# A residual block on one core: nesting the columns of the last chunk's outer row positions, with merged nesting and output operations

## Chip, cores and metric

The kernel runs on one core of a Trainium2 chip. The metric is the device time of one execution in microseconds, as a median of several executions.

## The reference

The block is GroupNorm, SiLU and a 3x3 convolution, done twice, with a time embedding added in between and the input added at the end. x is 2 x 512 x 64 x 64, all data bf16.

```python
def reference(x, t_emb, g1, be1, w1, w_emb, g2, be2, w2):
    ...
    h = conv3(_silu(gn(x, g1, be1)), w1)         # 3x3, 512 -> 512 channels
    emb = _silu(t_emb) @ w_emb
    h = h + emb.reshape(B, C, 1, 1)
    h = conv3(_silu(gn(h, g2, be2)), w2)
    return x + h
```

## The kernel before

The work is cut into eight *chunks*, one for each layer (0 or 1), image and half image; chunks 0 to 3 are layer 0, chunks 4 to 7 layer 1. A chunk has four *units*, one for each block of 128 output channels, named here by chunk and block: unit 5,3 is the last of chunk 5. While TensorE works on the units of chunk c, VectorE and ScalarE produce the operands of chunk c+1 (`prod`: load, SiLU, transforms).

Rows are transformed so that four output rows come from six *row positions*: the inner ones 0 to 3 and the outer ones 4 and 5. For each position and each of the four input-channel blocks (`ct`) the column direction is done in one of two ways:

- plain: three matmuls of 512 columns, one for each column of the 3x3 filter;
- *nested*: the columns are transformed as well. Four matmuls of 256 columns are left, two of them (`B_mms`) on sums and two (`A_mms`) on differences. This asks VectorE for the differences and sums (the four nesting operations below) and for sums of the weights.

In chunks 4 to 7 the inner positions are nested and the outer ones plain, with weights that are streamed in for each unit.

```python
def plain_mms(bank, c, k, ct, s):                 # 3 matmuls x 512 columns
    ...
def B_mms(bank, c, k, ct, s):                     # 2 x 256, on the sums
    ...
def A_mms(bank, c, k, ct, s):                     # 2 x 256, on the differences
    ...
# rows_b: the nesting of one input-channel block (nf = 2 or 4 positions)
X = lambda i: A(xb + i, [[RW, 8 * nf], [1, 32]])
for kind, (i, j, op) in enumerate(((32, 33, SB_), (1, 0, SB_), (33, 0, SB_), (33, 0, AD))):
    s0 = vnest(c, ct, kind, 0)
    tt(A(s0, [[1, 256 * nf]]), X(i), X(j), op, nm)
```

A unit of chunks 4 to 7, and what every unit does after its matmuls:

```python
p1, p2, p3, p4 = next_pair(), next_pair(), next_pair(), next_pair()   # PSUM bank pairs, 3 in turn
run([(6, 4, plain_mms)]);  evac_o(4, 6)                   # outer: banks 6 and 7
run([(p1, 0, B_mms), (p1 + 1, 2, B_mms)]);  evac_b(0, p1)  # ScalarE empties PSUM
run([(7, 5, plain_mms)]);  evac_o(5, 7)
run([(p2, 1, B_mms), (p2 + 1, 3, B_mms)]);  evac_b(1, p2)
s_ops()                                                   # VectorE
run([(p3, 0, A_mms), (p3 + 1, 2, A_mms)]);  evac_pair(0, p3)
run([(p4, 1, A_mms), (p4 + 1, 3, A_mms)]);  evac_pair(1, p4)
... # sums into MB and SD
yr = lambda r0: A(ys + r0 * RW, [[RW, 16], [33, 2], [1, 32]])
tt(yr(0),  A(MB, [[0, 2], [1, 512]]), A(MB + 1024, [[512, 2], [1, 512]]), AD, nm + "y")     # reads MB
tt(yr(16), A(SD, [[0, 2], [1, 512]]), A(SD + 1024, [[-512, 2], [1, 512]]), AD, nm + "y")    # reads SD
```

Almost everything in on-chip memory lies in one tile, the *arena* `ar`; `A(offset, dims)` is a strided view of it (offsets in f16 elements of a partition).

```python
Z    = 60096   # scratch; SD0 = Z + 10016 (chunks 0-3), SD1 = Z + 12768 (chunks 4-7), O0 at Z + 11552
VB1  = 74944   # operands of the odd chunks
AB   = 91584   # the two row buffers: loads of x and h land here, SiLU works on them in place
YS   = 96004   # the two output buffers
MB   = 100164  # inner sums
```

The order on each engine is not written by hand. Each operation is registered with a `Plan`, which keeps the exact set of elements that it reads and writes, finds the dependencies from those sets, and makes a list schedule with a cost model of its own. The operations are then emitted in that order, and the framework below inserts the semaphore waits, by its own reading of the views:

```python
def op(self, eng, cost, fn, r=(), w=(), ...):
    for sp, idx in r: deps.update(np.unique(self.spaces[sp][0][idx]).tolist())   # exact elements
    ...
def emit(self):
    for o in sorted(self.ops, key=lambda o: (o.start, o.i)): o.fn()
```

## Time and profile before

| | before |
|---|---|
| time, median of 3 | 476.97 us (476.17 to 478.6) |
| span of the profiled execution | 474.9 us |
| TensorE busy, VectorE busy | 461.3, 428.2 us |
| TensorE's gaps after its opening 10 us | 4.2 us (1.26 + 1.72 + 0.86 + 0.32) |
| from TensorE's last matmul to the end of the span | 4.8 us |

The page of the profile: busy time of each engine (PE is TensorE, DVE VectorE, ACT ScalarE), the clock granted to TensorE in 40 slices, and the chain that ended last.

```profile
span 474.9 us, 8229 instructions
...
PE 461.3 (97%) x2936; PEld 283.4 (60%) x2936; DVE 428.2 (90%) x847; ACT 371.9 (78%) x580; POOL 38.8 (8%) x66
...
PEclk9998999999999999999999999999999999999999
...
PE 40%; DVE 24%; ACT 7%; issue 4%; POOL 0%; DVEq 0%; ACTq 0%; POOLq 0%
```

The timeline of TensorE, the stretches that begin after an idle time: start, length, operation, and in brackets the idle time before it and its releaser (the wait for the first load at the start is left out).

```profile
37.12 13.14 PE L379 MATMUL psum<-ar 128*128 128x512 f16 x51 [1.26 <-DVE ar L328]
91.86 12.15 PE L379 MATMUL psum<-ar 128*128 128x512 f16 x60 [1.72 <-ACT ar L351]
177.10 111.05 PE L379 MATMUL psum<-ar 128*128 128x512 f16 x642 [0.86 <-DVE fs L441]
289.49 180.64 PE L379 MATMUL psum<-ar 128*128 128x512 f16 x1292 [0.32 <-DVE fs L441]
```

TensorE is the limit: it runs without a gap from 289.5 to 470.1 us. It is also the largest part of the chain (40%, on the page); VectorE's 24% lie before 289.5 us and after 457.9 us, in the output work of the last unit. L328 is the helper for VectorE's two-operand operations, L351 the one for ScalarE, and L379 the one for matmuls.

Busy times in the first one and a half units of chunk 7 and in the rest of it: window, its length, busy us and count of PE, PEld, DVE, ACT and POOL, TensorE's clock, DMA share and GB/s.

```profile
420.00:439.00 19.00, 19.00 (x132) 12.65 (x130) 14.07 (x22) 12.21 (x16) 2.65 (x3) 1.00 0.53 116
439.00:475.00 36.00, 31.13 (x230) 22.26 (x228) 20.75 (x40) 14.58 (x17) 3.61 (x3) 1.00 0.42 82
```

VectorE is 74% busy in the first window (14.07 of 19 us) and 58% in the second (20.75 of 36): in chunk 7 there is room to give VectorE work that takes columns off TensorE. Two groups of VectorE operations by shape: count, busy us, mean ns, idle before them.

```profile
L328 DVE TENSOR_TENSOR ar<-ar 128x1024 f16<-128x1024 f16 x272 | 179.1, 692 | 11.4 <-ACT ar L351 10.7
...
L328 DVE TENSOR_TENSOR ar<-ar 128x2048 f16<-128x2048 f16 x15 | 18.3, 1219 | 7.0 <-ACT ar L351 7.0
```

The Trainium skill ("VectorE: DVE Perf Modes", the perf-mode tier table) has 1224 ns for a bf16 `tensor_tensor` of 2048 elements; these f16 ones take 1219, so the trace agrees. "Perfetto Trace Analysis" (Optimizing Scalar/DVE Operations) names an overhead of about 60 ns for each VectorE operation on on-chip memory and says that larger operations help an engine that is saturated. That is the case for merging two of 1024 into one of 2048.

### The profile page before, as it was taken

What the parts mean: (1) busy time and instruction counts of PE and PEld (TensorE: products, weight loads), DVE (VectorE), ACT (ScalarE), POOL (GpSimd) and SP (SyncE); (2) the same over time, 40 slices, a digit from 0 to 9 for tenths busy, and PEclk for the clock granted to TensorE, in tenths of its full rate; (3) what the DMA queues carried; (4) which work ended last, traced back from release to release, by engine and by line L of the source; (5) the groups of instructions that cost most, each with busy time, mean ns of one, the idle gap of its engine ahead of it and who ended that gap; (6) DMA issues with size and microseconds to landing.
All of it is one profiled execution on the core that took longest, in us unless ns stands there. A gap on an engine that the chain in (4) does not pass through costs nothing.

```text
span 474.9 us, 8229 instructions
## 1 busy us (share of the span) xinstructions
PE 461.3 (97%) x2936; PEld 283.4 (60%) x2936; DVE 428.2 (90%) x847; ACT 371.9 (78%) x580; POOL 38.8 (8%) x66
## 2 busy tenths in 40 slices
PE   6998999899999999999999999999999999999995
PEld 5753555455555545555555576666666666677783
DVE  1699999999999999988999999998999999996447
ACT  5878999899999777689988778768776788655452
POOL 4100000010000000100000001104011111111111
PEclk9998999999999999999999999999999999999999
DMA  8943566366252466664775886685778487366534
GB/s 326 373 160 109 159 203 190 96 223 219 94 172 77 179 187 201 184 235 159 253 259 197 290 273 214 166 225 135 200 184 227 100 251 190 117 128 138 112 46 90
DMA packets 40505, 87.18 MB, mean 184 GB/s; under 512 B 6416, under 2 KB 14480, under 8 KB 40464
## 3 DMA queue, kind: packets, MB, share of 16 engines
q1 hardware_dynamic: 35520, 77.60, 48.5%
q0 software_dynamic: 4656, 9.05, 12.3%
q8 instruction: 23, 0.38, 0.3%
q14 instruction: 18, 0.15, 0.1%
q10 hardware_dynamic: 288, 0.01, 0.0%
HBM read 62.25 MB, written 31.32 MB: 197 GB/s over the span
## 4 chain that ended last, share of the span: by engine, by line
PE 40%; DVE 24%; ACT 7%; issue 4%; POOL 0%; DVEq 0%; ACTq 0%; POOLq 0%
PE psum L379 40%; DVE ar L328 22%; ACT ar L351 7%; DVE ar L332 2%; POOL fs L450 0%; POOL ar L364 0%; DVEq L1176 0%; DVE fs L441 0%; DVE fs L914 0%; DVE fs L915 0%; DVE fs L452 0%; DVE fs L917 0%; DVE fs L921 0%; DVEq L328 0%; ACTq L351 0%
## 5 line engine op out<-in xcount | busy, mean ns | idle before, releaser
L379 PE MATMUL psum<-ar 128*128 128x512 f16 (+2 forms) x2729 | 443.7, 325 | 4.3 <-ACT ar L351 1.7
L328 DVE TENSOR_TENSOR ar<-ar 128x1024 f16<-128x1024 f16 (+5 forms) x689 | 404.0, 648 | 27.4 <-ACT ar L351 24.2
L379 PEld LDWEIGHTS <-ar 128*128 128x128 f16 (+1 forms) x2765 | 266.6, 98 | 175.2 <-issue 7.4
L351 ACT ACTIVATE ar<-psum 128x512 f16<-128x512 f32 (+2 forms) x224 | 156.5, 714 | 53.3 <-PE psum L379 44.7
L351 ACT ACTIVATE ar<-ar 128x512 f16<-128x512 f16 (+6 forms) x185 | 158.1, 890 | 31.2 <-DVE ar L328 30.2
L351 ACT ACTIVATE ar<-ar,fs 128x2112 f16<-128x2112 bf16 (+1 forms) x32 | 68.7, 2149 | 6.8 <-DVE fs L454 2.9
L364 POOL DMA_DIRECT2D out_dram<-ar x15 | 18.1, 1207 | 115.9 <-DVE ar L328 91.8
L332 DVE TENSOR_SCALAR ar<-ar 128x512 f16<-128x512 f16 (+2 forms) x73 | 26.4, 381 | 0.5 <-ACT ar L351 0.5
L379 PE MATMUL psum<-ar,ones_bf 128*128 128x260 bf16 x128 | 18.3, 284 | 4.5 <-DMA ar<-in_x_dram 4.5
L351 ACT ACTIVATION_READ_ACCUMULATOR ar<-psum 128x1 f32 x100 | 20.8, 208 | 0.0
L379 PEld LDWEIGHTS <-ones_bf 128*128 128x128 bf16 x128 | 12.6, 100 | 9.9 <-issue 3.2
L450 POOL TENSOR_TENSOR fs<-fs 128x1 f32<-128x1 f32 (+1 forms) x7 | 9.0, 1281 | 108.9 <-DVE fs L448 97.2
L368 POOL MEMSET ar<- 128x65 f16 (+5 forms) x28 | 4.4, 197 | 121.8 <-PE psum L379 29.5
L364 POOL DMA_DIRECT2D ar<-ar x4 | 3.7, 924 | 79.2 <-DVE ar L328 63.8
L351 ACT ACTIVATION_READ_ACCUMULATOR ar<-ar 128x1 f32 x36 | 7.1, 198 | 0.0
L441 DVE COPY fs<-psum 128x2 f32<-128x2 f32 (+1 forms) x7 | 1.1, 158 | 4.7 <-PE psum L379 4.7
L967 DVE SCALAR_TENSOR_TENSOR ar<-psum,ident 128x128 bf16<-128x128 f32 x4 | 1.2, 290 | 4.6 <-PE psum L379 4.6
L379 PEld LDWEIGHTS psum<-fs,ones_neg 128*128 128x128 f32 x36 | 4.6, 191 | 0.8 <-issue 0.3
L379 PE MATMUL psum<-fs,ones_neg 128*128 128x1 f32 (+3 forms) x36 | 4.7, 244 | 0.1
L452 DVE TENSOR_TENSOR fs<-fs 128x1 f32<-128x1 f32 (+1 forms) x7 | 1.1, 157 | 2.2 <-POOL fs L450 2.1
L415 ACT ACTIVATE s_sb<-tparm 128x18 bf16<-128x18 bf16 x1 | 0.2, 218 | 3.1 <-DMA tparm<-in_t_emb_dram 3.1
L410 ACT ACT_TABLE_LOAD x1 | 1.3, 1283 | 1.7 <-PEq L1165 1.7
(40 smaller groups left out, 17.9 us busy)
## 6 DMA issues: line engine op xcount, KB each, us to landing
ar<-in_w_dram SPq DMA_DIRECT2D x32, 384.0 KB, 3.9
ar<-in_x_dram SPq DMA_DIRECT2D x16, 552.5 KB, 3.9
h_scr<-ar SPq DMA_DIRECT2D x16, 520.0 KB, 3.4
ar<-h_scr SPq DMA_DIRECT2D x16, 520.0 KB, 3.9
out_dram<-in_x_dram SPq DMA_DIRECT2D x30, 260.0 KB, 4.7
out_dram<-ar POOLq DMA_DIRECT2D x15, 520.0 KB, 5.8
u_scr<-ar SPq DMA_DIRECT2D x16, 384.0 KB, 2.8
ar<-u_scr SPq DMA_DIRECT2D x4, 1536.0 KB, 7.0
```

The costliest lines, as they stand in the source:

```text
L328: pl.op("DVE", 0.075 + 0.000521 * out.n, lambda: nc.vector.tensor_tensor(out=out.ap, in0=a.ap, in1=b.ap, op=op), regs(a, b), regs(out), name)
L332: pl.op("DVE", cost or 0.075 + 0.00026 * out.n, lambda: nc.vector.tensor_scalar(out=out.ap, in0=a.ap, scalar1=s, scalar2=None, op0=ALU.mul ...
L351: lambda: nc.scalar.activation(out=out.ap, in_=a.ap, func=func, scale=sc, **kw), regs(*rr), regs(*ww), name)
L364: lambda: eng.dma_start(out=out, in_=in_, **kw), regs(*r), regs(*w), name, lat=3.2 if sw else None, after=after, sw=sw)
L368: pl.op("POOL" if eng == "gpsimd" else "DVE", 0.08 + 0.0005 * out.n, lambda: e.memset(out.ap, v), (), regs(out), name)
L379: nc.tensor.matmul(out.ap, lhsT=lhsT.ap, rhs=rhs.ap, start=st, stop=sp, skip_group_check=True)
L410: nc.scalar.activation(out=fs[:, WARM:WARM + 1], in_=fs[:, WARM + 1:WARM + 2], func=ACT.Silu)
L415: nc.scalar.activation(out=s_sb[:], in_=tparm[:], func=ACT.Silu)
L441: pl.op("DVE", 0.16, lambda: V.tensor_copy(out=F(tot, 2 * n).ap, in_=ps.ap), regs(ps), regs(F(tot, 2 * n)), name)
L450: pl.op("POOL", 0.85, lambda: nc.gpsimd.tensor_tensor(out=F(rs, n).ap, in0=N.ap, in1=F(NEGH, n).ap, op=ALU.pow), regs(N), regs(F(rs, n)), ...
L452: small(lambda: V.tensor_mul(out=S.ap, in0=F(rs, n).ap, in1=F(g, n).ap), [F(rs, n)], [S], name)
L967: pl.op("DVE", 0.3, lambda: nc.vector.scalar_tensor_tensor(out=j2.ap, in0=g.ap, scalar=1.0 / HW, in1=ident[:], op0=ALU.mult, op1=ALU.mult, ...
```

## The change

There are three parts.

1. Chunk 7 nests the outer positions too. A unit's 24 outer matmuls of 512 columns become 32 of 256. VectorE gets the nests of the outer positions, and in every unit the sums of the streamed weights (`nest_st`). The outer sets now come last in the unit, and chunk 7 uses four bank pairs in turn.
2. In all nested chunks, four nesting operations become three: the first two kinds are done by one operation of twice the size.
3. In all chunks, the two output operations `y` become one. Its operands have an outermost stride of `SD - MB`: the first half of the result reads MB, the second SD. For that, the places of M(2) and M(3) are swapped.

```diff
@@ rows_b
-        for kind, (i, j, op) in enumerate(((32, 33, SB_), (1, 0, SB_), (33, 0, SB_), (33, 0, AD))):
-            s0 = vnest(c, ct, kind, 0)
-            tt(A(s0, [[1, 256 * nf]]), X(i), X(j), op, nm)
+        X2 = lambda i, j: A(xb + i, [[j - i, 2], [RW, 8 * nf], [1, 32]])
+        tt(A(vnest(c, ct, 0, 0), [[1, 512 * nf]]), X2(32, 1), X2(33, 0), SB_, nm)
+        for kind, op in ((2, SB_), (3, AD)):
+            tt(A(vnest(c, ct, kind, 0), [[1, 256 * nf]]), X(33), X(0), op, nm)
+        if c == 7:
+            ... # the same for positions 4 and 5: one operation of 1024, two of 512
@@ new
+    def nest_st(s, nm):                       # sums of the streamed weights, once a unit
+        ...
+        tt(t, g(0), g(2), ALU.add, nm)
+        tt(A(LV + 4160 + s * 1024, ...), t, g(1), ALU.add, nm)
+        tt(g(1, None), t, g(1), ALU.subtract, nm)
+    def unit7(c, k):
+        pr = lambda: next_pair(4)
+        p1, p2, p3, p4, p5, p6 = pr(), pr(), pr(), pr(), pr(), pr()
+        nest_st(u % 2, nm + "n")
+        ... # inner positions as in unit(), then
+        run([(p5, 4, Bo_mms), (p5 + 1, 5, Bo_mms)])
+        ... # evictions, sums
+        run([(p6, 4, Ao_mms), (p6 + 1, 5, Ao_mms)])
+        ... # evictions, output with two adds for the outer positions
@@ unit (chunks 0 to 6)
-        scal(se[0], M(2), M(1), 8.0, nm + "8")
-        scal(se[1], M(3), M(1), 2.0, nm + "2")
+        scal(se[0], M(3), M(1), 8.0, nm + "8")
+        scal(se[1], M(2), M(1), 2.0, nm + "2")
-        yr = lambda r0: A(ys + r0 * RW, [[RW, 16], [33, 2], [1, 32]])
-        tt(yr(0), A(MB, [[0, 2], [1, 512]]), A(MB + 1024, [[512, 2], [1, 512]]), AD, nm + "y")
-        tt(yr(16), A(SD, [[0, 2], [1, 512]]), A(SD + 1024, [[-512, 2], [1, 512]]), AD, nm + "y")
+        tt(A(ys, [[RW, 32], [33, 2], [1, 32]]), A(MB, [[SD - MB, 2], [0, 2], [1, 512]]),
+           A(MB + 1536, [[SD - MB - 512, 2], [-512, 2], [1, 512]]), AD, nm + "y")
```

More of the change, by code (lines that the diff above doesn't have):

```diff
@@ L569, in vplane @@
             return v + 2048 + {1: 0, 3: 1, 4: 2, 5: 3}[s] * PL
+        if c == 7:
+            return X1 + s * PL
         return VX[c % 2] + ct * 1088 + (s - 4) * PL
@@ L576, in vnest, with onest @@
         return v + kind * 1024 + s * 256
+    ONEST = [Z + 7440, TB, None, None]
+    LV = VB[0]
+    def onest(ct, kind, s):
+        return ONEST[ct] + kind * 512 + (s - 4) * 256
     def load_a(c, ct, resident=None):
@@ L659, in rows_b @@
         X = lambda i: A(xb + i, [[RW, 8 * nf], [1, 32]])
-        for kind, (i, j, op) in enumerate(((32, 33, SB_), (1, 0, SB_), (33, 0, SB_), (33, 0, AD))):
-            s0 = vnest(c, ct, kind, 0)
-            tt(A(s0, [[1, 256 * nf]]), X(i), X(j), op, nm)
+        X2 = lambda i, j: A(xb + i, [[j - i, 2], [RW, 8 * nf], [1, 32]])
+        tt(A(vnest(c, ct, 0, 0), [[1, 512 * nf]]), X2(32, 1), X2(33, 0), SB_, nm)
+        for kind, op in ((2, SB_), (3, AD)):
+            tt(A(vnest(c, ct, kind, 0), [[1, 256 * nf]]), X(33), X(0), op, nm)
+        if c == 7:
+            if ONEST[ct] is None:
+                ONEST[ct] = ab
+            xb += 4 * PL
+            Y2 = lambda i, j: A(xb + i, [[j - i, 2], [RW, 16], [1, 32]])
+            tt(A(onest(ct, 0, 4), [[1, 1024]]), Y2(32, 1), Y2(33, 0), SB_, nm)
+            for kind, op in ((2, SB_), (3, AD)):
+                tt(A(onest(ct, kind, 4), [[1, 512]]), A(xb + 33, [[RW, 16], [1, 32]]), A(xb, [[RW, 16], [1, 32]]), op, nm)
     ucnt = [0]
@@ L667, with next_pair @@
     prs = [0]
-    def next_pair():
+    def next_pair(n=3):
         prs[0] += 1
-        return 2 * ((prs[0] - 1) % 3)
+        return 2 * ((prs[0] - 1) % n)
     SSUM = {}
@@ L710, in A_mms, with Bo_mms, Ao_mms @@
         return lst
+    def Bo_mms(bank, c, k, ct, s):
+        lst = []
+        for q in range(2):
+            w = (A(LV + 4160 + ucnt[0] % 2 * 1024 + ct * 256 + (s - 4) * 128, [[1, 128]]) if q == 0 else
+                 A(st_off(ucnt[0] % 2, ct) + (s - 4) * 384 + 128, [[1, 128]]))
+            lst.append((Ps(bank, q * 256, [[1, 256]]), w, A(onest(ct, 3 - q, s), [[1, 256]]),
+                        ct == 0 and q == 0, ct == CT - 1 and q == 1))
+        return lst
+    def Ao_mms(bank, c, k, ct, s):
+        lst = []
+        for q in range(2):
+            w = A(st_off(ucnt[0] % 2, ct) + (s - 4) * 384 + q * 256, [[1, 128]], BF16)
+            lst.append((Ps(bank, q * 32, [[64, 8], [1, 32]]), w, A(onest(ct, q, s), [[1, 256]]),
+                        ct == 0 and q == 0, ct == CT - 1 and q == 1))
+        return lst
@@ new lines, in nest_st, with run, evac_b, evac_pair @@
+    def nest_st(s, nm):
+        g = lambda kx, dt=BF16: A(st_off(s, 0) + kx * 128, [[2 * UM - UM, 2], [384, 4], [1, 128]], dt)
+        t = A(LV + 3136, [[512, 2], [128, 4], [1, 128]])
+        tt(t, g(0), g(2), ALU.add, nm)
+        tt(A(LV + 4160 + s * 1024, [[512, 2], [128, 4], [1, 128]]), t, g(1), ALU.add, nm)
+        tt(g(1, None), t, g(1), ALU.subtract, nm)
+    def unit7(c, k):
+        nm = f"u{c}{k}"
+        u = ucnt[0]
+        ufirst[u] = len(pl.ops)
+        ys = YS[u % 2]
+        last = u == 31
+        BT, SD = BT1, SD1
+        BO, OS, OA = LV, LV + 1024, LV + 2064
+        M = lambda i, n=1, st=512: A(MB + i * 512, [[st, n], [1, 512]]) if n > 1 else A(MB + i * 512, [[1, 512]])
+        pr = lambda: next_pair(4)
+        p1, p2, p3, p4, p5, p6 = pr(), pr(), pr(), pr(), pr(), pr()
+        def run(steps):
+            for (bank, s, fn) in steps:
+                for ct in range(CT):
+                    mm(fn(bank, c, k, ct, s), nm + f"{fn.__name__[0]}{s}")
+        def evac_b(s, bank):
+            act(A(BT + s * 512, [[1024, 2], [1, 512]]), Ps(bank, 0, [[512, 2], [1, 512]]), ACT.Copy, scale=0.5 * KAP[s], name=nm + "b")
+        def evac_pair(s, bank):
+            act(M(s, 2, 1024), Ps(bank, 0, [[512, 2], [1, 512]]), ACT.Copy, scale=KAP[s], name=nm + f"m{s}")
+        row = lambda base, r0, dt=None: A(base + r0 * RW, [[RW, 8], [33, 2], [1, 32]], dt)
+        nest_st(u % 2, nm + "n")
+        run([(p1, 0, B_mms), (p1 + 1, 2, B_mms)])
+        evac_b(0, p1)
+        run([(p2, 1, B_mms), (p2 + 1, 3, B_mms)])
+        evac_b(1, p2)
+        g = lambda q: A(BT + q * 256, [[512, 4], [32, 8], [1, 32]])
+        for o, op in ((0, AD), (32, SB_)):
+            tt(A(SD + o, [[512, 4], [64, 8], [1, 32]]), g(0), g(1), op, nm + "S")
+        run([(p3, 0, A_mms), (p3 + 1, 2, A_mms)])
+        evac_pair(0, p3)
+        run([(p4, 1, A_mms), (p4 + 1, 3, A_mms)])
+        evac_pair(1, p4)
+        run([(p5, 4, Bo_mms), (p5 + 1, 5, Bo_mms)])
+        for i, sc in enumerate((0.5, 0.125)):
+            act(A(BO + i * 512, [[1, 512]]), Ps(p5 + 1 - i, 0, [[1, 512]]), ACT.Copy, scale=sc, name=nm + "b")
+        g = lambda q: A(BO + q * 256, [[512, 2], [32, 8], [1, 32]])
+        for o, op in ((0, AD), (33, SB_)):
+            tt(A(OS + o, [[PL, 2], [RW, 8], [1, 32]]), g(0), g(1), op, nm + "So")
+        run([(p6, 4, Ao_mms), (p6 + 1, 5, Ao_mms)])
+        act(row(OA, 8), Ps(p6, 0, [[1, 512]]), ACT.Copy, scale=0.25, name=nm + "o4")
+        if last:
+            last_y(c, k, M, SD, OS, OA, p6 + 1)
+            return
+        act(row(OA, 0), Ps(p6 + 1, 0, [[1, 512]]), ACT.Copy, name=nm + "o5")
+        tt(M(0, 4), M(0, 4), A(SD, [[512, 4], [1, 512]]), AD, nm + "A")
+        tw = lambda off, st: A(off, [[st, 2], [1, 512]])
+        tt(tw(SD, 512), M(0, 2), M(2, 2), AD, nm + "s")
+        tt(M(0, 2), M(2, 2), M(0, 2), SB_, nm + "d")
+        se = CFG["s"][c]
+        scal(se[0], M(3), M(1), 8.0, nm + "8")
+        scal(se[1], M(2), M(1), 2.0, nm + "2")
+        scal(se[2], A(SD + 1024, [[1, 512]]), A(SD + 512, [[1, 512]]), 4.0, nm + "4")
+        tt(A(ys, [[RW, 32], [33, 2], [1, 32]]), A(MB, [[SD - MB, 2], [0, 2], [1, 512]]),
+           A(MB + 1536, [[SD - MB - 512, 2], [-512, 2], [1, 512]]), AD, nm + "y")
+        yo = A(ys, [[24 * RW, 2], [1, PL]])
+        tt(yo, yo, A(OS, [[PL, 2], [1, PL]]), AD, nm + "O")
+        tt(yo, yo, A(OA, [[PL, 2], [1, PL]]), AD, nm + "O")
+        yv = A(ys, [[1, YF]])
+        b, ch = chunks[c][1:]
+        dma(out[b, k, ch], yv.ap, [yv], [K("o", b, k, ch, i) for i in range(2)], P * YF * 2, nm + "out", sw=True, acc=True)
+        ucnt[0] += 1
@@ L712, in unit @@
     def unit(c, k, opening=0):
+        if c == 7:
+            return unit7(c, k)
         l, b, ch = chunks[c]
@@ L770, in unit @@
             return [lambda: evac_o(4, 2 * k), lambda: evac_o(5, 2 * k + 1)]
-        if last:
-            return last_unit(c, k, run, evac_b, evac_pair, evac_o, s_ops, M, SD, OO)
         if md == "N":
@@ L827, in unit @@
         se = CFG["s"][c]
-        scal(se[0], M(2), M(1), 8.0, nm + "8")
-        scal(se[1], M(3), M(1), 2.0, nm + "2")
+        scal(se[0], M(3), M(1), 8.0, nm + "8")
+        scal(se[1], M(2), M(1), 2.0, nm + "2")
         scal(se[2], A(SD + 1024, [[1, 512]]), A(SD + 512, [[1, 512]]), 4.0, nm + "4")
-        yr = lambda r0: A(ys + r0 * RW, [[RW, 16], [33, 2], [1, 32]])
-        tt(yr(0), A(MB, [[0, 2], [1, 512]]), A(MB + 1024, [[512, 2], [1, 512]]), AD, nm + "y")
-        tt(yr(16), A(SD, [[0, 2], [1, 512]]), A(SD + 1024, [[-512, 2], [1, 512]]), AD, nm + "y")
+        tt(A(ys, [[RW, 32], [33, 2], [1, 32]]), A(MB, [[SD - MB, 2], [0, 2], [1, 512]]),
+           A(MB + 1536, [[SD - MB - 512, 2], [-512, 2], [1, 512]]), AD, nm + "y")
         yo = A(ys, [[24 * RW, 2], [1, PL]])
@@ L849, in unit, with last_x, last_y @@
         ucnt[0] += 1
-    def last_unit(c, k, run, evac_b, evac_pair, evac_o, s_ops, M, SD, OO):
+    def last_x(k):
+        l, b, ch = chunks[7]
+        d = A(VB[0] + 16640, [[1, YF]], BF16)
+        dma(d.ap, x[b, k, ch][:, RW:RW + YF], [], [d], P * YF * 2, "ulx")
+    def last_y(c, k, M, SD, OS, OA, bank):
         l, b, ch = chunks[c]
         nm = "ul"
-        ys, yb, dx = YS[1], VB[0], VB[0] + 2112
-        xt = AB[acnt[0] % 2]
-        d = A(xt, [[1, YF]], BF16)
-        dma(d.ap, x[b, k, ch][:, RW:RW + YF], [], [d], P * YF * 2, nm + "x")
+        ys, yb, dx, xt = YS[1], LV + 6272, LV + 8384, VB[0] + 16640
         memz("gpsimd", A(yb + 32, [[RW, 32], [1, 1]], BF16), nm)
-        p1, p2, p3, p4 = next_pair(), next_pair(), next_pair(), next_pair()
-        run([(p1, 0, B_mms), (p1 + 1, 2, B_mms)])
-        evac_b(0, p1)
-        run([(p2, 1, B_mms), (p2 + 1, 3, B_mms)])
-        evac_b(1, p2)
-        s_ops()
-        run([(p3, 0, A_mms), (p3 + 1, 2, A_mms)])
-        evac_pair(0, p3)
-        run([(p4, 1, A_mms), (p4 + 1, 3, A_mms)])
-        evac_pair(1, p4)
-        run([(6, 4, plain_mms)])
-        evac_o(4, 6)
-        run([(7, 5, plain_mms)])
         tw = lambda off, st: A(off, [[st, 2], [1, 512]])
@@ L893, in last_unit @@
         tt(row(ys, 0), one(dx), M(1), AD, nm + "y")
-        tt(row(yb, 24, BF16), row(ys, 24), row(OO[0], 0), AD, nm + "O")
+        yo = A(ys, [[24 * RW, 2], [1, PL]])
+        tt(yo, yo, A(OS, [[PL, 2], [1, PL]]), AD, nm + "O")
+        tt(row(yb, 24, BF16), row(ys, 24), row(OA, 8), AD, nm + "O")
         st(24, 8)
-        o5 = Ps(7, 0, [[1, 512]])
+        o5 = Ps(bank, 0, [[1, 512]])
         pl.op("DVE", 0.68, lambda: nc.vector.tensor_tensor(
@@ L1090 @@
                     memz("gpsimd", A(UREG[j] + 9728 + 32, [[RW, 8], [1, 1]]), "oz")
+            if c == 7 and k == 0:
+                for base in (LV + 1024, LV + 2064):
+                    memz("gpsimd", A(base + 32, [[RW, 16], [1, 1]]), "oz")
+            if c == 7 and k == 3:
+                last_x(k)
             if l == 1:
```

## The prediction

> **What bounds it now.** The page gives TensorE 461.3 of 474.9 us (97%), VectorE 428.2 (90%). The chain of waits is TensorE alone from 289.5 to 457.9 us, then VectorE and ScalarE to the end. In windows of the last two chunks TensorE is 100% busy up to 470.1 us; VectorE is 99% busy to about 420 us but only 40-60% in chunk 7. Starts in the trace: a 256-column matmul takes 0.109 us, a 512-column one 0.2225, so a unit of chunk 7 is 24 x 0.2225 + 64 x 0.109 = 12.3 us, and its units do start 12.33 us apart (420.7, 433.0, 445.3). The Trainium skill ("TensorE: Matmul & The Clock Gate", Back-to-back issue gap) gives N/2.4 + 2.5 ns, 109 and 216: the trace agrees.
>
> **TensorE term.** The 24 512-column outer matmuls become 32 of 256 columns: 96 x 0.109 = 10.5 us a unit, 1.85 us less, 7.4 us over four units if all lay on the critical path. It doesn't:
>
> **Tail.** In the last unit of before the four nested inner sets end at 464.7 us, and the plain outer sets (5.4 us) run while VectorE works through the output chain to 472.1; the span ends 2.8 later. That chain (7.4 us from the end of the inner sets) isn't shortened; it gains two sum operations and a 1040-element add. So the last unit's 1.85 us buys nothing: TensorE merely ends 3.8 instead of 2 us before VectorE. I give +0.2 us for the added work.
>
> **VectorE term.** Durations: 1024 elements 0.61 us back to back, 2048 1.13, 512 0.34. Added: outer nesting 4 x 1.3, weight sums 4 x 1.8, outer output adds about 1.3 a unit; saved by merging about 0.1 us per pair of 1024-element operations. From the order of operations with these durations VectorE has 417 -> 430 us of work. Most falls into chunk 7's idle time. The merged order moves production forward: the last nests needed by chunk 7's first matmuls lie at 383.0 us of cumulative VectorE work, against 383.1 before, so production isn't late (ready about 418.6, needed about 421.3). But the outer nests and weight sums stand before the output of units 6,3: its last output add shifts from 391.4 to 396.1 of cumulative work.
>
> **New wait.** Chunk 7 now starts with nested sets on a bank pair that still holds unit 6,3's first inner pair. Its eviction started at 421.8 us before, while TensorE wants the bank at 420.7: I expect a stall of 1-2 us at the start of chunk 7 (eviction after about 421, plus 1.0), and perhaps 0.3 us more at its second unit. From there VectorE has about 9 us per 10.5 us unit: no further stall.
>
> **Sum.** 3 x 1.85 = 5.5 gained, -1.7 stall, -0.2 tail: about 3.7 us. The TensorE gaps before (1.3, 1.7, 0.9, 0.3 us at 36, 90, 176, 289 us) can move either way by 1 us.
>
> Predicted 473.2 us, 470.3 to 476.0; faster by over 2%: 0.05, within 2%: 0.93, slower: 0.02.
>
> **Right if:** units of chunk 7 are 10.5 us apart; one TensorE wait on ScalarE near 421 us; VectorE busy 12-14 us more; the span ends about 6.5 us after TensorE (4.8 before). **Wrong if:** VectorE falls behind in chunks 5-6 and TensorE waits for nests (slower); or the bank is evicted in time and the early gaps close (470).

## More of the kernel before

Waits by engine, line and what was waited for: us in total, times, longest.

```profile
ACT ar L351 <- PE psum L379: 44.7, 55, 2.0
ACT ar L351 <- DVE ar L328: 34.8, 35, 3.2
...
PE psum L379 <- ACT ar L351: 1.7, 1, 1.7
```

ScalarE waits mostly for TensorE, as it should where TensorE is the limit, and TensorE waits for ScalarE once.

## The result, and the profile after

| | before | after |
|---|---|---|
| time, median (range) of 4 runs | 476.83 us (476.17 to 478.6) | 491.13 us (490.49 to 491.29) |
| span of the profiled execution | 474.9 us | 489.4 us |
| TensorE busy, VectorE busy | 461.3, 428.2 us | 458.4, 442.7 us |
| TensorE's gaps after the opening | 4.2 us | 19.2 us |
| from TensorE's end to the end of the span | 4.8 us | 7.1 us |

The ratio is 1.029, with a 95% interval of 1.026 to 1.032. A ratio is always the mean time of one kernel's fast runs over the mean of the other's of the same rounds, so it isn't quite the ratio of the medians quoted. Executions over 1.5% slower than the fastest of the same kernel are left out of the means. The change is 14 us slower where 3.7 us were expected to be won.

The page after, the same lines:

```profile
span 489.4 us, 8261 instructions
...
PE 458.4 (94%) x2968; PEld 288.1 (59%) x2968; DVE 442.7 (90%) x824; ACT 373.3 (76%) x588; POOL 37.7 (8%) x68
...
PEclk9999999799999999999999998999999999999999
...
DVE 2%; DVEq 0%; issue 0%
```

The clock dips in two slices, early and in the middle. The chain is of no use here: it could be followed back only through VectorE's last operations, 2% of the span. TensorE's stretches after a gap, from 80 us on:

```profile
85.58 8.91 PE L379 MATMUL psum<-ar 128*128 128x512 f16 x27 [5.35 <-ACT ar L351]
185.17 105.54 PE L379 MATMUL psum<-ar 128*128 128x512 f16 x604 [3.31 <-DVE fs L441]
293.14 7.12 PE L379 MATMUL psum<-ar 128*128 128x256 f16 x38 [2.43 <-ACT ar L351]
...
424.03 14.23 PE L379 MATMUL psum<-ar 128*128 128x256 f16 x104 [1.42 <-ACT ar L351]
438.96 10.64 PE L379 MATMUL psum<-ar 128*128 128x256 f16 x96 [0.70 <-ACT ar L351]
450.68 31.60 PE L379 MATMUL psum<-ar 128*128 128x256 f16 x288 [1.07 <-ACT ar L351]
```

The last two lines are chunk 7, and they are nearly what was predicted: a unit takes 10.64 us in one piece (10.5 predicted), and the two stalls are 0.70 + 1.07 = 1.8 us (1.7 predicted). But chunk 7 starts at 438.96 us. In before it started at 420.66. The loss lies before the part that the prediction worked on: TensorE's unit ends are already 5.8 us later than before's at the end of chunk 0, 12.1 us at the end of chunk 3 and 15.9 us at the end of unit 6,0.

Waits after:

```profile
ACT ar L351 <- DVE ar L328: 69.5, 43, 4.8
...
PE psum L379 <- ACT ar L351: 13.8, 8, 5.3
ACT ar L351 <- PE psum L379: 13.8, 23, 1.9
```

ScalarE's waits for VectorE doubled, from 34.8 to 69.5 us, and its waits for TensorE fell from 44.7 to 13.8; TensorE waits for ScalarE 13.8 us instead of 1.7. The direction has turned round: VectorE holds ScalarE, which holds TensorE.

Two windows after the gap at 80 us, and the second of the two windows shown for before (chunk 7 in both kernels):

```profile
85.60:88.80 3.20, 3.20 (x8) 1.11 (x8) 3.08 (x5) 3.20 (x8) 0.00 (x0) 0.50 0.46 107
88.80:92.30 3.50, 3.50 (x11) 1.26 (x10) 3.43 (x8) 3.44 (x8) 0.00 (x0) 0.64 0.52 200
...
439.00:475.00 36.00, 34.92 (x319) 31.06 (x319) 34.24 (x57) 23.54 (x32) 4.81 (x4) 1.00 0.57 119
```

VectorE is now 95% busy in the last window (34.24 of 36 us), yet no gap but the two shown occurs in chunk 7. After the gap of 5.35 us TensorE runs at half clock (0.50) for 3.2 us and at 0.64 for another 3.5. The Trainium skill ("TensorE: Matmul & The Clock Gate", Part 1, What's actually happening, and HAM oscillation) says that idle gaps over about 3.4 us make the clock fall to half, until TensorE has been busy for about as long. That agrees for this gap: 17 matmuls of 512 columns took 6.68 us, where starts 0.2225 us apart and the last one's own 0.39 us would make 3.95. But the length of a gap alone doesn't decide: after the gap of 2.43 us at 290.7 the clock was 0.61 over 3.9 us, and after the 3.31 us at 181.9 it was not lowered (9 matmuls in 2.16 us).

The trace shows why. Its two half-clock spells begin at 84.52 and at 292.73 us, which is 61 steps of 3.413 us apart, and they last two such steps and one (0.50 from 292.73 to 296.14 us; the 0.61 is a mean over half and full clock). The three spells of y_merge, a run described below, begin at 178.8, 294.9 and 410.9 us, 34 such steps apart. So the clock changes on a grid of 3.413 us, and a gap counts by what it takes out of one step. The gap of 2.43 us took 2.03 us out of the step from 289.32 to 292.73; that of 3.31 us lay across the edge at 183.50 and took 1.65 and 1.66 us out of two. Idle time isn't all of it: in before the clock was 0.50 from 37.84 to 41.24 us after a gap of only 1.26 us, with 36 matmuls of two columns each (1.04 us) just before the gap.

The span's 14.5 us thus come together as: -7.4 from fewer columns, +4.5 left over, for the most part the lower clock (busy time changed by -2.9 in all; the two spells cost about 2.7 and 1.5 us, but before's own spell cost 1.6, so this term isn't fully accounted for), +15.0 from gaps (19.2 - 4.2) and +2.3 from the later end of VectorE. What must be explained is the gaps, and with them the clock.

The 2048-element operations, nests and merged outputs among them:

```profile
L328 DVE TENSOR_TENSOR ar<-ar 128x2048 f16<-128x2048 f16 x62 | 76.6, 1236 | 17.7 <-DMA ar<-in_x_dram 5.9 <-ACT ar L351 5.8 <-DMA ar<-ar 4.4
```

They take no longer (1236 ns) but wait longer, and for odd things: 5.9 us for loads of x, which no operation of this shape reads, and 4.4 us for an accumulating transfer between operand planes.

### The profile page after: what moved, and what is told of

Read it like the earlier page. It is cut to its first block, busy times and chain, and to the rows that moved or that the text cites. A ratio compares the mean times of both kernels' runs of the same rounds, so it can differ in the third digit from the quotient of the medians.

```text
span 489.4 us, 8261 instructions
## 1 busy us (share of the span) xinstructions
PE 458.4 (94%) x2968; PEld 288.1 (59%) x2968; DVE 442.7 (90%) x824; ACT 373.3 (76%) x588; POOL 37.7 (8%) x68
## 5 line engine op out<-in xcount | busy, mean ns | idle before, releaser
L379 PE MATMUL psum<-ar 128*128 128x256 f16 (+2 forms) x2761 | 440.2, 321 | 19.3 <-ACT ar L351 13.8
L328 DVE TENSOR_TENSOR ar<-ar 128x1040 f16<-128x1040 f16 (+8 forms) x666 | 418.1, 686 | 27.2 <-ACT ar L351 11.6
L379 PEld LDWEIGHTS <-ar 128*128 128x128 f16 (+1 forms) x2797 | 271.0, 99 | 182.3 <-issue 25.5
L351 ACT ACTIVATE ar<-ar 128x384 bf16<-128x384 bf16 (+6 forms) x185 | 158.7, 895 | 46.1 <-DVE ar L328 42.4
L351 ACT ACTIVATE ar<-psum 128x512 f16<-128x512 f32 (+2 forms) x232 | 159.2, 711 | 40.0 <-DVE ar L328 17.8
L379 PEld LDWEIGHTS <-ones_bf 128*128 128x128 bf16 x128 | 12.9, 102 | 10.5 <-issue 3.3
L368 POOL MEMSET ar<- 128x65 f16 (+6 forms) x30 | 4.5, 197 | 162.3 <-issue 48.7
L450 POOL TENSOR_TENSOR fs<-fs 128x1 f32<-128x1 f32 (+1 forms) x7 | 7.6, 1092 | 106.9 <-DVE fs L448 106.9
```

Of the source, the lines that this page charges most:

```text
L328: pl.op("DVE", 0.075 + 0.000521 * out.n, lambda: nc.vector.tensor_tensor(out=out.ap, in0=a.ap, in1=b.ap, op=op), regs(a, b), regs(out), name)
L351: lambda: nc.scalar.activation(out=out.ap, in_=a.ap, func=func, scale=sc, **kw), regs(*rr), regs(*ww), name)
L368: pl.op("POOL" if eng == "gpsimd" else "DVE", 0.08 + 0.0005 * out.n, lambda: e.memset(out.ap, v), (), regs(out), name)
L379: nc.tensor.matmul(out.ap, lhsT=lhsT.ap, rhs=rhs.ap, start=st, stop=sp, skip_group_check=True)
L450: pl.op("POOL", 0.85, lambda: nc.gpsimd.tensor_tensor(out=F(rs, n).ap, in0=N.ap, in1=F(NEGH, n).ap, op=ALU.pow), regs(N), regs(F(rs, n)), ...
```

## Experiments

Two theories were formed at first. The *order theory*: with fewer and larger VectorE operations the planner found another order, good by its own costs and bad on the chip. The *merged-operation theory*: one of the merged operations itself brings waits, whatever the order. The expectations name a rival of both, the *VectorE-load theory*: the added nests and sums make VectorE the limit. Fourteen kernels were run. All results were correct. "Before" in brackets is the median of the kernel before in the same call.

### First call: pin the order (before 477.08 us, 7 runs)

In these four the emission order is fixed to a recorded one; operations without a counterpart keep their planned place, and a merged operation stands at the later place of its two halves.

```diff
-        for o in sorted(self.ops, key=lambda o: (o.start, o.i)):
-            o.fn()
+        for i in ORDER:            # recorded from the other kernel
+            self.ops[i].fn()
```

**before_ops_after_order**: all operations of before, in the order of the changed kernel (chunks 0 to 6).

> The arithmetic of the kernel before, unchanged, but every engine gets its instructions in the order that the scheduler chose for the changed kernel (chunk 7's own units keep their order). Order theory: the 17 us that the changed kernel had lost by the start of chunk 7 come from the instruction order of chunks 0 to 6 alone, so this one loses most of them though nothing was added: 485 to 492 us, with a TensorE gap of some 5 us near 80 us (waiting for ScalarE) and a half-speed clock after it. Merged-operation theory (fewer, longer operations that wait for more inputs and hold buffers longer are what costs): the operations are unmerged here, so below 481 us. VectorE-load theory (the added outer nests and sums make VectorE the limit): 475 to 479 us.

Measured: 477.04 us, ratio 0.9994 (0.9944 to 1.0045). The order alone costs nothing. The order theory falls.

**after_before_order**: the changed kernel in before's order.

> All of the change, but the instructions of chunks 0 to 6 in the order of the kernel before. Order theory: the gap at 80 us and the long ones at 182 and 291 us go, chunk 7 starts within about 3 us of 420.7 and the run takes 470 to 475 us. Merged-operation theory: the merged operations stay, so most of the loss stays: above 482 us. VectorE-load theory: the early gaps go, but chunk 7 starts about 5 us late: 476 to 480 us.

Measured: 505.75 us, ratio 1.0594 (1.0542 to 1.0646). Before's order doesn't help; it is 15 us worse than the order that the planner found for the changed operations. Only the merged-operation theory's range holds it.

**c7_before_order**: the nesting of chunk 7 alone, with merges undone in rows_b and in the units of chunks 0 to 6, in before's order.

> Chunk 7's nested outer positions without any merging in chunks 1 to 6, in the order of the kernel before. Order theory: 471 to 475 us. Merged-operation theory: also about 472 to 475 us, since nothing is merged outside chunk 7. VectorE-load theory: chunk 7 starts 4 to 5 us late, 476 to 480 us.

Measured: 482.29 us, ratio 1.0106 (1.0057 to 1.0155), above the ranges of all three theories. TensorE waited 5.69 us at chunk 7's start for an eviction by ScalarE, which had itself waited for VectorE (1.72 us, to 429.3); an order made for other work doesn't fit the added operations. This says little about part 1 itself.

**merge_before_order**: only the two merges, in before's order.

> Only the merged nesting and output operations, in the order of the kernel before; chunk 7 as before. Order theory: 475 to 478 us, VectorE about 5 us less busy. Merged-operation theory: 482 us or more, with TensorE gaps in chunks 0 to 3 where an inner eviction waits for the merged output operation. VectorE-load theory: as before or 1 us faster.

Measured: 501.77 us, ratio 1.0509 (1.0458 to 1.0561). The merges alone, in an order that gave 477 us without them, cost 25 us, with no work added to VectorE. The merged-operation theory stands, the VectorE-load theory doesn't explain this loss.

### Second call: one part at a time, with a free schedule (before 476.0 us, 7 runs)

**y_merge**: before with part 3 alone.

```diff
-        tt(yr(0), A(MB, [[0, 2], [1, 512]]), A(MB + 1024, [[512, 2], [1, 512]]), AD, nm + "y")
-        tt(yr(16), A(SD, [[0, 2], [1, 512]]), A(SD + 1024, [[-512, 2], [1, 512]]), AD, nm + "y")
+        tt(A(ys, [[RW, 32], [33, 2], [1, 32]]), A(MB, [[SD - MB, 2], [0, 2], [1, 512]]),
+           A(MB + 1536, [[SD - MB - 512, 2], [-512, 2], [1, 512]]), AD, nm + "y")   # and M(2), M(3) swapped
```

> The kernel before with only the two output operations of a unit merged into one (chunks 0 to 6, and 7 but for its last unit); the scheduler orders it freely. The order theory has fallen. Merged-output theory (the one output operation can start only when all three scaled operands are there, and frees the four inner-sum buffers only at its end, so evictions behind it and the output's successors come later): 485 us or more, VectorE waiting for ScalarE more than the 24 us of before, TensorE gaps ending with an eviction. Merged-nest theory (the double-length nesting operation is what delays): 475 to 479 us.

Measured: 506.38 us, ratio 1.0637 (1.0621 to 1.0653). One merge of two small operations costs 30 us.

**nest_merge**: before with part 2 alone (the first hunk of the diff above, without `if c == 7`).

> The kernel before with only the first two nesting operations merged (chunks 1 to 7), scheduled freely. Merged-output theory: 475 to 478 us, VectorE 2 to 3 us less busy. Merged-nest theory: 485 us or more.

Measured: 476.87 us, ratio 1.0018 (1.0003 to 1.0033): 0.9 us slower, next to nothing. VectorE's busy time is 0.5 us less (427.7), not 2 to 3.

**c7_nest**: the full change with part 3 undone in chunks 0 to 6 (chunk 7's own output operation stays merged).

> The changed kernel with only the merged output operation of chunks 0 to 6 undone (chunk 7 keeps its own), scheduled freely. Merged-output theory: the loss in chunks 0 to 4 goes, what is left is chunk 7's gain of about 5 us less VectorE's backlog before it: 471 to 479 us. Merged-nest theory: 485 us or more, as the changed kernel.

Measured: 471.31 us, ratio 0.9898 (0.9882 to 0.9915). This beats both kernels. TensorE is busy 453.9 us, its gaps are 3.7 us, and the span ends 7.5 us after it.

**c7_only**: as c7_nest, with part 2 undone too.

> Chunk 7's nested outer positions with no merging in chunks 0 to 6, scheduled freely. Merged-output theory: 472 to 479 us, within 2 us of the run with the merged nests. Merged-nest theory: 472 to 477 us, and more than 8 us below the run with the merged nests.

Measured: 478.06 us, ratio 1.0042 (1.0024 to 1.0059). That is in the range, but not within 2 us of c7_nest as the merged-output theory had it. The merged nests, worth nothing alone, make a difference of 6.8 us beside chunk 7's nesting: without them TensorE waits 1.86 + 1.50 us around 423 us. Why is not shown: they save VectorE only 1.5 us of busy time (443.9 and 442.4), so the order that the planner finds may matter more.

So the output merge is the culprit. But why? The merged operation takes the same time anywhere (below). In y_merge something else is seen. The timeline of all engines around one of its gaps:

```profile
407.95 2.57 DVE L328 TENSOR_TENSOR ar<-ar 128x2048 f16<-128x2048 f16 x3 [2.76 <-DMA ar<-h_scr]
409.21 2.15 ACT L351 ACTIVATE ar<-ar,fs 128x2112 f16<-128x2112 f16 x1 [4.41 <-DVE ar L328]
...
411.27 1.92 ACT L351 ACTIVATE ar<-psum 128x1024 f16<-128x1024 f32 x2
...
412.32 0.58 PE L379 MATMUL psum<-ar 128*128 128x256 f16 x2 [5.69 <-ACT ar L351]
```

The first operation of the first line is the merged output of unit 5,3 (1.226 us, so it ends at 409.18). It waited 2.76 us for a load of h into a row buffer. It reads MB and SD and writes an output buffer, so it has nothing to do with that load. The second line is a SiLU of chunk 7, which works on a row buffer. It starts 0.04 us after the merged output ends, after 4.41 us of idling. It has nothing to do with the output either. Then come the PSUM evictions that it had delayed, and TensorE after 5.69 us without work.

This gave a further theory, *false waits*. The merged view has two pieces that lie `SD - MB` apart, about 30,050 elements in chunks 0 to 3 and 27,300 in chunks 4 to 7. If whoever inserts the waits takes the view as everything from its first to its last element, then the operation "reads" all that lies between SD and MB: the outer eviction buffers (chunks 0 to 3), the odd chunks' operands, the row buffers and the output buffers. Whoever writes there next must wait for it, and it must wait for whoever wrote there last. The planner, with exact elements, sees none of this. In the semaphore waits of the built programs (counted there, not in a trace) 13 ScalarE instructions of y_merge wait for a merged output with which they share no element, and 11 of the changed kernel; before has no merged output.

### Third call: take away the distance (before 476.4 us, 11 runs)

The merged operation stays as it is, but SD lies directly below MB, so that nothing is between them. To make room the output buffers move into the scratch.

```diff
-    VB = [o, o + 16640 + 2240 + 14848]
+    VB = [o, o + 16640 + 2240 + 14912]
-    o += 33280 + 2240 + 14848
+    o += 33280 + 2240 + 14912
-    YS = [o, o + YF];  o += 2 * YF
+    YS = [Z + 10720, Z + 10720 + YF];  NB = o;  o += 4096
     MB = o
-    BT0 = Z + 8992;  SD0 = Z + 10016;  O0 = [Z + 11552, Z + 12592, Z + 13632]
+    BT0 = NB;  SD0 = NB + 2560;  O0 = [Z + 8192, Z + 9232, NB + 1024]
-    BT1 = Z + 10720;  SD1 = Z + 12768
+    BT1 = NB;  SD1 = NB + 2048
```

**y_merge_near**: y_merge in this layout.

> The merged output operation alone (as in the run that took 506 us) with one difference: the arena is laid out anew so that the sums' buffer lies directly below the inner-sum buffers. Same instructions, same true dependencies, other addresses. False-wait theory: the merged operation reads two places 27,000 to 30,000 elements apart as one strided operand; the dependency tracking treats the whole stretch between them as read, so in the 506 us run evictions and activations that write there waited for it, and it for them (the trace has them starting 0.1 us after its end). With nothing in between these waits go: 474 to 479 us. True-wait theory (the operation needs all three scaled operands at once and holds the inner sums longer): 495 us or more.

Measured: 476.34 us, ratio 0.9994 (0.9964 to 1.0025), against 1.0637 for the same operations in the old layout. The cost of the merge is gone.

**before_near**: before (split output) in this layout, as a control.

> Control: the kernel before in the new arena layout, nothing merged. Both theories: 475 to 478 us.

Measured: 476.04 us, ratio 0.9983 (0.9956 to 1.0009). The layout in itself does nothing.

The 2048-element operations of y_merge, then of y_merge_near (the lines of the helpers are one higher there):

```profile
L328 DVE TENSOR_TENSOR ar<-ar 128x2048 f16<-128x2048 f16 x46 | 56.2, 1223 | 34.8 <-ACT ar L351 12.1 <-issue 10.6 <-DMA ar<-in_x_dram 6.7
```

```profile
L329 DVE TENSOR_TENSOR ar<-ar 128x2048 f16<-128x2048 f16 x46 | 56.1, 1219 | 11.4 <-ACT ar L352 11.3
```

The operation takes the same time (1223 and 1219 ns), so a wide stride is not slow in itself. The idle time before them falls from 34.8 to 11.4 us, and the waits for loads of x are gone. The waits of ScalarE for VectorE, y_merge and y_merge_near:

```profile
ACT ar L351 <- DVE ar L328: 66.2, 49, 5.3
```

```profile
ACT ar L352 <- DVE ar L329: 28.7, 29, 3.0
```

They fall from 66.2 us to 28.7; before had 34.8. TensorE's gaps (after the opening) are 26.8 us in y_merge and 3.8 us in y_merge_near, and its busy time is 467.3 and 460.4 us (the lower clock after gaps): 23.0 + 6.9 = 29.9 us, all of the difference of the spans (504.2 and 474.4). VectorE's busy time is 1.7 us less than in before_near (426.4, 428.1) for 31 operations fewer, 55 ns each. This is what the skill's 60 ns promised, and all that the merge can give.

**after_near**: the full change in this layout.

> All of the change, in the new arena layout. False-wait theory: the whole loss goes; as the change with the output operation split, 469 to 473 us. True-wait theory: 485 us or more.

Measured: 474.88 us, ratio 0.9962 (0.994 to 0.9985). This is above the expected 469 to 473 us. The false waits account for about 16 us of the changed kernel's 491.1 (the two times are of different calls, with before at 476.8 and 476.4), and without them the change is 0.4% faster than before. TensorE's stretches after a gap, from chunk 5 on:

```profile
289.71 131.34 PE L380 MATMUL psum<-ar 128*128 128x512 f16 x940 [1.41 <-DVE fs L442]
421.83 10.64 PE L380 MATMUL psum<-ar 128*128 128x256 f16 x96 [0.78 <-ACT ar L352]
433.50 31.60 PE L380 MATMUL psum<-ar 128*128 128x256 f16 x288 [1.04 <-ACT ar L352]
```

There is no gap from 289.7 to 421.0 us, and at chunk 7 stand the two predicted stalls, 0.78 and 1.04 us.

**after_near_banks**: after_near with chunk 7's bank pairs moved on by two, so that its first matmuls find another bank pair.

```diff
         pr = lambda: next_pair(4)
+        if k == 0:
+            prs[0] += 2
```

> As the last, and chunk 7's first unit starts two bank pairs further on, so that its first nested sets do not go to the pair that still holds the inner sums of the unit before (the stall that the prediction put at 1 to 2 us). False-wait theory: 0.5 to 2 us below the last, 467.5 to 472 us; if VectorE's backlog and not the bank sets the start of chunk 7, no difference. True-wait theory: 485 us or more.

Measured: 474.7 us, ratio 0.9955 (0.9934 to 0.9976). The expected gain of 0.5 to 2 us didn't come. The first stall is gone (as the prediction's account of the bank says), but the second is 1.97 instead of 1.04 us: what limits chunk 7's start is not only the bank but also the buffer MB, which the output of unit 6,3 must have read before it can be written again. In the trace that output ends at 432.28 us, the eviction of the second unit starts at 432.38 and TensorE at 433.45. No net gain.

### Fourth call: what the merged output still costs (before 476.24 us, 11 runs)

after_near (474.9) is slower than c7_nest (471.3), which has the split output in the old layout.

**c7_nest_near**: c7_nest in the near layout. It differs from after_near by the output merge alone.

> The whole change in the new arena layout, but with the output operation of chunks 0 to 6 split again. It differs from the 474.9 us run by the split alone, and from the 471.3 us run by the layout alone. If a merged output still costs something once its false waits are gone (it needs three scaled operands at once and frees the inner sums later): 470 to 472.5 us. If the layout costs it (or the order that the scheduler finds for it): 474 to 476 us.

Measured: 471.37 us, ratio 0.9892 (0.9871 to 0.9914). The layout costs nothing here either; the merged output costs 3.5 us in this company, though alone it cost 0.3, within the noise (y_merge_near against before_near). TensorE's unit ends part at a wait of 1.41 us at 288 us for a GroupNorm statistic of VectorE (the first line above) and at chunk 7's first stall of 0.78 us, neither of which c7_nest_near has (it waits 2.15 us for another such statistic, before 102.8 us, where after_near waits 0.29). The merged operation needs MB and SD both, so it starts at the later of two readiness times, and the planner makes another order around it. Which of the two makes the difference was not told apart.

**c7_nest_banks**: c7_nest with the same two lines as in after_near_banks.

> The 471.3 us version (old layout, split output, nested outer positions and merged nests) with chunk 7 starting two bank pairs further on. There the first unit of chunk 7 started without a gap and the second one waited 1.3 us for the inner-sum buffers, not for a bank, so if that is what bounds it: 470.5 to 472 us, no difference; if banks do: 469 to 470.5 us.

Measured: 471.23 us, ratio 0.9889 (0.9867 to 0.991): no difference; the second unit of chunk 7 still waits 1.14 us.

| profiled run | TensorE busy | gaps | end of TensorE to end | span |
|---|---|---|---|---|
| before | 461.3 | 4.2 | 4.8 | 474.9 |
| after | 458.4 | 19.2 | 7.1 | 489.4 |
| after_near | 453.8 | 6.7 | 7.7 | 472.8 |
| c7_nest | 453.9 | 3.7 | 7.5 | 469.9 |

## Why the prediction was wrong

Point by point:

- *TensorE term, right.* "96 x 0.109 = 10.5 us a unit, 1.85 us less": units of 10.64 us. Where the clock isn't lowered after the opening, in the near layout, TensorE's busy time falls by 7.3 us (from 461.1 in before_near to 453.8 in after_near), 7.4 predicted.
- *New wait, right in kind, its sum by luck.* "a stall of 1-2 us at the start of chunk 7 ... and perhaps 0.3 us more at its second unit": 0.70 + 1.07 us in after and 0.78 + 1.04 in after_near. The sum is 1.8 for 1.7, but only because two errors cancel: the first stall is smaller than forecast and the second over three times larger, because the second unit waits for MB. after_near_banks shows it.
- *Tail, right in kind, too small.* The end was to lie 6.5 us after TensorE's; it lies 7.1 us after it, and 7.7 in after_near.
- *VectorE term, slightly small in size.* 12 to 14 us more busy time; measured 14.5 (12.8 in the near layout: 440.9 in after_near, 428.1 in before_near).
- *Production isn't late, right once the false waits are gone.* after_near has no gap in chunks 5 and 6. In after TensorE waits several times there, but for ScalarE.
- *The failed step:* "saved by merging about 0.1 us per pair of 1024-element operations", and beside it "The TensorE gaps before ... can move either way by 1 us". The merged output was counted as a saving and nothing else, in all 28 units before chunk 7, and the part of the span before chunk 7 was taken as unchanged. The saving itself was about half of the forecast (55 ns for each merged output). What was missing is a cost of another kind. The dependencies were taken from the planner, which keeps exact elements, while the waits of the built program come from a reading of the views in which a view over two far places touches what lies between. TensorE's gaps went from 4.2 to 19.2 us, and its clock fell after some of them.

The chance given to "slower" was 0.02. With the distance taken away the same operations take 474.9 us, inside the predicted range of 470.3 to 476.0; the 16 us between are the part that the prediction had no term for. Even so the gain over before is then 1.5 us (476.4 to 474.9), less than half of the 3.7 forecast, because the merged output still costs 3.5 us beside the other parts.

What is shown: the merge costs 30 us alone, and the cost goes when the two buffers lie side by side, with the operation and its duration unchanged and a control that excludes the layout. That the waits come from the stretch between the pieces is shown by that, by the merged outputs' waits for loads that they don't read, and by the SiLU that starts 0.04 us after an output that it doesn't share. One thing changed beside the addresses: the planner's order. In the traces of y_merge and y_merge_near VectorE's operations differ in kind or shape at 138 of 816 places, and no run put y_merge's order into the near layout. Against order as the cause stands merge_before_order, which lost 25 us in an order that takes 477 us without the merges; and in the built programs of y_merge_near and after_near, counted as above, no ScalarE instruction waits for a merged output with which it shares no element. What is not shown is which single false wait makes which gap of the changed kernel. The gap at 80 us, for instance, ends after a stretch in which ScalarE was busy nearly throughout (5.09 of 5.40 us), so it may be a late effect of earlier waits. Also open are the last 3.5 us between after_near and c7_nest_near.

## What to carry to other kernels

Don't join two operations by a stride over two far-apart buffers before you have looked at which waits the built program gets: a saving of 55 ns an operation was paid with 30 us of waits, and moving the buffers side by side took the cost away. A planner that knows exact elements says nothing about waits that another layer inserts; a group that waits for a load it doesn't read is the sign of it in a profile. When a change has several parts, run each alone: here the version without the output merge (471.3 us) beats the kernel before by 1% and the full change by 4%.

## What the Trainium skill lacked or had wrong

- No page says that an operand in two far-apart pieces can make a program wait for all that lies between. It belongs to "Perfetto Trace Analysis", Optimizing Scalar/DVE Operations, as a limit to its advice to group operations: 506.4 us with the pieces some 27,300 to 30,050 elements apart, 476.3 us side by side.
- "TensorE: Matmul & The Clock Gate", Part 1, HAM oscillation: a limit of about 3.4 us for an idle gap is too lenient. A gap of 5.35 us was followed by a clock of 0.50, but so was one of 2.43 us, for 3.41 us, and one of 3.31 us was not. What the same part says of a free-running window of about 3.4 us fits the trace's grid of 3.413 us; what it lacks is that a window need not be idle throughout: in the trace of after 2.03 us of it were enough and 1.66 were not.
- The same page, Back-to-back issue gap: it gives about 131 ns for each matmul of 512 columns in a stream of weight loads and matmuls, and calls N/2.4 + 2.5 (216 ns) an over-count. Here, in such a stream, starts are 222 ns apart (109 ns for 256 columns, as by the formula), so the formula is nearer.
